# Turning q and k by squares on VectorE instead of whole on TensorE, from the ninth attention block on

## The chip, the cores and the metric

The kernel runs on one core of a Trainium2 chip. The metric is the device time of one launch in microseconds. The median of three runs before the change is 1019.25 us (1018.29 to 1020.09). A profile of one execution is read beside it; in it, all times count from the start of that execution's span.

## What is computed

Four batches of eight heads, 576 positions and 64 features per head go through window attention, and its output, 2304 tokens of 512 features, through two gated MLPs one after the other.

```python
scores = scale * np.matmul(q, k.transpose(0, 1, 3, 2))
mask = (rel >= 0) & (rel < 64)            # rel = query position - key position
attn = softmax(np.where(mask, scores, -1e9))
x = attn @ v                              # then (B, H, S, D) -> (B*S, H*D)
x = (silu(x @ w_gate) * (x @ w_val)) @ w_out
out = (sigmoid(x @ w2_gate) * (x @ w2_val)) @ w2_out
```

Everything is held to float32. The weights are 512 x 1536 and 1536 x 512 and arrive as float64 words, which the kernel rounds on the chip.

## The kernel before

The tokens are cut into 18 attention blocks of 128 tokens, numbered from 0, and into five tiles of 4, 3, 4, 4 and 3 blocks (`BLOCKS`). A tile of four blocks gives products of 512 columns, a tile of three blocks 384. The first MLP goes over the five tiles in turn, then the second MLP does. Each pass over a tile has twelve feature chunks, and each chunk three **slots**: the gate product (`g`, L402), the value product (`v`, L402) and the output product of the chunk before (`a`, L414). A product is twelve matmuls, since both operands are split into a high and a low float32r part. There are 36 slots to a tile, 360 in all.

The order around the products is written out by hand: three tables, `before`, `during` and `after`, hold for every slot what is issued ahead of its product, behind it and at its end. The instructions of each engine then run in that order, and each waits only for its operands and buffers. The attention of the first tile's blocks is done ahead of all products (`START`). The attention of every later block is spread over the slots of the tile before it by `plan_attention(i, base, ...)`; `base` is a gate slot, and the blocks of a tile are 9 or 12 slots apart. For one block it plans:

- slot `base - 2`: `load_qk`, the block's q and k, 128 tokens by 8 heads by 64 features each, from main memory into one buffer each (pool `nat`);
- `base + 1`, `base + 5`: v of the block, and a second tile `v0` that `pair_v` puts together by two copies within on-chip memory, from the v tiles of this block and the one before;
- ahead of the value product of slot `base + 1`: `transpose_in` for q and for k. Each is four TensorE transposes of 128 x 128 against an identity matrix (L183), into a PSUM bank. `evacuate` copies them out on ScalarE into `qt` (L192) and `kt` (L198); `kt` has 64 keys more, copied from the block before (L198);
- ahead of slot `base + 2`: the scores, 32 small matmuls (L217) that read `qt` and `kt`; then mask, exponentials and normalization, the transposes of the probabilities (L275), the product with v (L291) in slot `base + 9` or `base + 10`, and its split into the next tile's input (`x_hi` on ScalarE L301, `x_lo` on VectorE L304).

`qt` and `v0` share one buffer: `v0` of a block waits for its scores, and `qt` of the next block for this block's product with v. Weights come as 512 KB pieces (`raw`, L332) into four buffers; ScalarE (L350, L353) and VectorE (L361 to L364) round them. All of the first MLP's are rounded during the first tile's slots, slots 0 to 35, those of the second during tiles 2 and 3. Nearly all transfers are issued by SyncE's queue (SP), in order.

Of the kernel before, what the change touches and what calls it, by code (L numbers as in the profile page):

```python
# [8 lines left out]
FP32 = mybir.dt.float32  # L9
# [9 lines left out]
# A float64's upper word, read as a float32, for the magnitudes 2**-127 and about 2**128.  # L19
# [3 lines left out]
# What comes before the products, in order. Loads: q, k, v and the block, r and the last of the  # L23
# weight chunks whose words are wanted by then, h for the q and k of the next tile's first block.
# [3 lines left out]
# Steps: two letters, then the block (attention) or the chunk (c., weights).  # L28
# [11 lines left out]
def attention_moe_moe(  # L40
# [32 lines left out]
    ORDER2 = [t for t in range(NTL) if t != last] + [last]  # L73
    TILES = []
# [38 lines left out]
    def load_tokens(src, nm, t0, pool):  # L113
        pool, tag = pool or (nat_p, nm)
        t = pool.tile([128, H, D], FP32, tag=tag, name=nm)
        for off, n, b, s in runs(t0, 128):
            nc.sync.dma_start(
                out=t[off:off + n], in_=src[b, :, s:s + n, :].rearrange("h p d -> p h d")
            )
        return t  # L120

    def load_qk(i, pool=None):
        nat[i, "q"] = load_tokens(q, "q", 128 * i, pool)
        nat[i, "k"] = load_tokens(k, "k", 128 * i, pool)
# [4 lines left out]
    def pair_v(i, pool=None):  # L129
        """The keys of the block's first half, then those of the half block before them."""  # L130
        pool, tag = pool or (qt_p, "qt")
        q_eng = nc.scalar if early[0] else nc.sync
        t = pool.tile([128, H, D], FP32, tag=tag, name="v0")
        q_eng.dma_start(out=t[0:W], in_=nat[i, "v1"][0:W])
        if i:
            q_eng.dma_start(out=t[W:], in_=nat[i - 1, "v1"][W:])
        else:
            nc.gpsimd.memset(t[W:], 0.0)
        nat[i, "v0"] = t
# [4 lines left out]
    def make_masks():  # L144
        for nm, firsts in (("n", ()), ("a", (0,)), ("b", (1,))):
            m = const.tile([128, 2 * W], FP32, name=f"mask_{nm}")
            nc.vector.memset(m, 0.0)
            for half in range(2):
                mh = m[half * W:(half + 1) * W]
                own, before = (slice(0, W), slice(W, 2 * W))[::1 - 2 * half]  # L150
# [37 lines left out]
    def evacuate(i, nm):  # L188
# [4 lines left out]
        else:  # L193
# [5 lines left out]
            if i == 0:  # L199
                nc.gpsimd.memset(t[:, :, 128:], 0.0)  # L200
            else:
                copy(t[:, :, 128:], st[i - 1, "kt"][:, :, W:128])
            copy(t[:, :, 0:128], ps)
        st[i, nm + "t"] = t

    def scores(i, picks=(None, None), pars=(0, 1)):
        """A quarter of the array per product, four different ones in a row."""
# [3 lines left out]
        thirds = kt.rearrange("p a (g w) -> p a g w", w=W)  # L211
        for hp in range(HP):
            for par, half in ((0, 0), (0, 1), (1, 0), (1, 1)):
                if par not in pars:
# [5 lines left out]
                    rhs=kt[r, hp, 0:2 * W] if half else thirds[r, hp, 0:3:2, :],  # L220
# [63 lines left out]
    def pv(i, pick=None):  # L284
        ps = bank(pick)
        pt = [st.pop((i, "pt", par)) for par in range(2)]
        vv = [nat.pop((i, "v0")), nat[i, "v1"]]
# [29 lines left out]
    def rows(key):  # L317
        """The part of a weight that one tile holds, its features on the partitions."""
# [21 lines left out]
    # A float64 is rounded to a float32 as the sum of two words. One is the upper word without  # L340
# [121 lines left out]
    def plan_attention(i, base, t, col):  # L462
# [250 lines left out]
```

## Time and profile before

| | before |
|---|---|
| median of three runs | 1019.25 us |
| the profiled execution's span | 1017.5 us |
| TensorE busy in the span | 992.6 us, 98% |
| VectorE, ScalarE busy | 501.9 us, 509.1 us |
| mean granted TensorE clock | 0.984 |
| packets moved by DMA | 115285, 106.21 MB |

The span is the time from the first to the last instruction of one execution. The timed runs include what lies around it, and the median stands 1.75 us above the span. Busy shares are means over stages that differ: in the first 155 us the weights are rounded beside the first tile, and the last half of the run is products alone.

### The profile page before, as it was taken

To read this page: it belongs to the slowest core of one execution; us is meant where nothing else is said; L and a number is where in the kernel's file an instruction comes from. 1 tells how busy PE (TensorE), PEld (TensorE's weight loads), DVE (VectorE), ACT (ScalarE), POOL (GpSimd) and SP (SyncE) were. 2 spreads that over 40 slices of the span, in tenths; PEclk is the share of its full clock that TensorE was granted. 3 is DMA by queue.
4 is the path that set the end of the run, shared out by engine and by line. 5 is a ranking of instruction groups with operands and counts; after the bars stand their busy time and mean duration, and the time that the engine had idled before them with its cause. 6 is when DMAs were issued, how large, how long until landed. Compare 5 with 4: busy or idle time off the path is not lost.

```text
span 1017.5 us, 14797 instructions
## 1 busy us (share of the span) xinstructions
PE 992.6 (98%) x5701; PEld 855.2 (84%) x5701; DVE 501.9 (49%) x1161; ACT 509.1 (50%) x1011; POOL 4.1 (0%) x20
## 2 busy tenths in 40 slices
PE   8799998999999999999999999999999999999998
PEld 6677777999878888888999888899988888888997
DVE  6899994444466766666555422233322222222322
ACT  6899994665676777657444322222222222222222
POOL 1000000000000000000000000000000000000000
PEclk7799999999999999999999999999999999999999
DMA  9647664622176665564555310020020002000100
GB/s 227 183 156 210 196 196 134 177 74 73 44 226 197 177 197 190 185 206 145 189 153 157 135 41 1 1 83 1 1 73 1 0 1 73 1 1 1 42 1 32
DMA packets 115285, 106.21 MB, mean 104 GB/s; under 512 B 61008, under 2 KB 87632, under 8 KB 115216
## 3 DMA queue, kind: packets, MB, share of 16 engines
q1 hardware_dynamic: 114656, 104.36, 34.5%
q10 hardware_dynamic: 560, 0.92, 0.4%
q8 instruction: 45, 0.74, 0.3%
q14 instruction: 24, 0.20, 0.1%
HBM read 78.64 MB, written 22.02 MB: 99 GB/s over the span
## 4 chain that ended last, share of the span: by engine, by line
PE 83%; ACT 10%; DVE 4%; issue 2%; DMA 0%; ACTq 0%; SPq 0%; DVEq 0%
PE a L414 26%; PE g L402 26%; PE v L402 25%; ACT raw L350 3%; ACT z L252 2%; PE att L291 1%; PE att L183 1%; PE att L217 1%; ACT t L353 1%; PE att L275 1%; DVE raw L361 1%; DVE t L363 1%; ACT wv L384 1%; ACT L252 1%; ACT wg L384 0%
## 5 line engine op out<-in xcount | busy, mean ns | idle before, releaser
L402 PE MATMUL g<-x,wg 128*128 128x512 f32 (+1 forms) x1440 | 319.6, 371 | 1.3 <-ACT x L301 1.3
L402 PE MATMUL v<-x,wv 128*128 128x512 f32 (+1 forms) x1440 | 318.4, 369 | 0.0
L402 PEld LDWEIGHTS g<-x,wg 128*128 128x128 f32 x1440 | 264.7, 189 | 38.6 <-ACT x L301 1.4
L402 PEld LDWEIGHTS v<-x,wv 128*128 128x128 f32 x1440 | 260.6, 188 | 32.6
L666 DVE TENSOR_TENSOR s<-s,v 128x512 f32<-128x512 f32 (+1 forms) x120 | 76.0, 633 | 339.7 <-PE v L402 323.5
L657 ACT ACTIVATE s<-g 128x512 f32<-128x512 f32 (+1 forms) x120 | 66.6, 555 | 303.7 <-PE g L402 303.4
L414 PE MATMUL a<-h,wo 128*128 128x512 f32 (+1 forms) x720 | 164.9, 377 | 6.4 <-DVE h L582 6.4
L414 PE MATMUL a<-wo,h 128*128 128x512 f32 x648 | 157.5, 391 | 0.0
L668 ACT ACTIVATE h<-s 128x512 fp32r<-128x512 f32 (+1 forms) x120 | 70.6, 588 | 167.6 <-DVE s L666 167.6
L414 PEld LDWEIGHTS a<-h,wo 128*128 128x128 f32 x720 | 131.1, 190 | 26.7 <-DVE h L582 7.7
L414 PEld LDWEIGHTS a<-wo,h 128*128 128x128 f32 x648 | 121.3, 188 | 24.1
L350 ACT ACTIVATE raw<-raw 128x512 uint16<-128x512 uint32 x72 | 97.9, 1360 | 0.0
L582 DVE TENSOR_TENSOR h<-s,h 128x512 fp32r<-128x512 f32 (+1 forms) x120 | 76.2, 635 | 3.2
L361 DVE TENSOR_SCALAR raw<-raw 128x512 uint16<-128x512 uint16 x72 | 54.2, 752 | 17.4 <-ACT raw L350 17.3
L252 ACT ACTIVATE z<-z,nm 128x128 f32<-128x128 f32 x144 | 55.8, 390 | 2.9 <-DVE nm L236 2.7
L100 DVE TENSOR_TENSOR x<-rx,x 128x512 fp32r<-128x512 f32 (+1 forms) x20 | 12.8, 639 | 84.6 <-ACT x L99 84.6
L364 DVE CUSTOM_DVE_ANT_0 t<-raw,t 128x1024 uint16<-128x1024 uint16 x72 | 49.9, 693 | 2.5
L353 ACT ACTIVATE t<-raw 128x512 f32<-128x512 f32 x72 | 51.1, 710 | 0.0
L388 DVE TENSOR_TENSOR wo<-stay,wo 128x512 fp32r<-128x512 f32 x60 | 41.1, 685 | 0.0
L384 ACT ACTIVATE wo<-stay 128x512 fp32r<-128x512 f32 x60 | 37.4, 623 | 0.0
L388 DVE TENSOR_TENSOR wo<-tw,wo 128x512 fp32r<-128x512 f32 x48 | 33.0, 687 | 5.7 <-ACT wo L384 5.7
L362 DVE TENSOR_SCALAR t<-t 128x512 f32<-128x512 f32 x72 | 33.5, 465 | 0.0
(82 smaller groups left out, 588.9 us busy)
## 6 DMA issues: line engine op xcount, KB each, us to landing
raw<-in_moe_w_gate_dram SPq DMA_DIRECT2D x24, 512.0 KB, 4.2
raw<-in_moe_w_val_dram SPq DMA_DIRECT2D x24, 512.0 KB, 4.0
raw<-in_moe_w_out_dram SPq DMA_DIRECT2D x24, 512.0 KB, 3.7
tw<-k0o SPq DMA_DIRECT2D x48, 256.0 KB, 4.4
out_dram<-o SPq DMA_DIRECT2D x18, 256.0 KB, 2.3
k<-in_k_dram SPq DMA_DIRECT2D x16, 256.0 KB, 5.1
q<-in_q_dram SPq DMA_DIRECT2D x16, 256.0 KB, 4.7
v<-in_v_dram SPq DMA_DIRECT2D x16, 256.0 KB, 5.1
```

The costliest lines, as they stand in the source:

```text
L252: nc.scalar.activation(out=z[:, hp, :], in_=z[:, hp, :], func=ACTF.Exp, scale=-1.0, bias=nm[:, hp:hp + 1], accum_out=su[:, hp:hp + 1],)
L350: nc.scalar.activation(out=first, in_=lower.bitcast(UINT32), func=ACTF.Copy, scale=2.0 ** -29)
L353: nc.scalar.activation(out=t.bitcast(FP32), in_=upper.bitcast(FP32), func=ACTF.Abs)
L361: nc.vector.tensor_scalar(second, fourth, 0x8000, 0x4000, ALU.bitwise_and, ALU.bitwise_or)
L364: nc.vector.tensor_tensor(out=t, in0=t, in1=lower, op=ALU.add)
L388: nc.vector.tensor_tensor(out=w[:, 1], in0=mids.pop(key), in1=w[:, 0].bitcast(FP32), op=ALU.subtract)
L402: nc.tensor.matmul(out=ps[:, 0:n], lhsT=w[:, a, c, :], rhs=xt[:, b, c, 0:n], start=(j == 0), stop=(j == len(mm) - 1),)
L414: nc.tensor.matmul(out=acc[e][:, 0:n] if m == 0 else acc[e], lhsT=w[:, a, cols] if m == 0 else h[:, a, cols], rhs=h[:, b, 0:n] if m == 0 e ...
L582: nc.vector.tensor_tensor(out=h[:, 1, 0:n], in0=s, in1=h[:, 0, 0:n].bitcast(FP32), op=ALU.subtract)
L657: nc.scalar.activation(out=s, in_=gps[:, 0:n], func=(ACTF.Silu, ACTF.Sigmoid)[m])
L666: nc.vector.tensor_tensor(out=s, in0=s, in1=vps[:, 0:n], op=ALU.mult)
L668: nc.scalar.activation(out=h[:, 0, 0:n], in_=s, func=ACTF.Copy)
```

## The change

Blocks 0 to 7 keep their TensorE transposes. For blocks 8 to 17 (`TURN` is 8), the tokens that they need are first copied within main memory: `to_squares` copies q and k in pieces of 32 features of one token into two arrays, `squares`, in which the 32 x 32 squares of the transposed layout stand where the whole transposed matrix would have them, each square still unturned. There are 96 such transfers: 32 of 32 x 6 pieces (batch 1, from its position 384 on), in slots 12 to 27; 32 of 32 x 18 pieces (batch 2) in slots 24 to 39; 32 of 32 x 18 (batch 3) in slots 46 to 61. A piece is 32 float32 values, 128 bytes. All are issued by SP, ahead of what else its slot issues.

The block's `load_qk` then reads q as 128 partitions by four runs of 512 bytes and k, with the 64 keys before the block, as four runs of 768 bytes. In slot `base + 1`, `turn` makes `qt` and `kt` by one VectorE transpose each, 128 x 512 and 128 x 768, which turns every 32 x 32 square in its place. The transposes on TensorE and the three copies out of PSUM on ScalarE fall away for these blocks.

Besides, for all blocks, `load_before` loads `v0` from main memory (128 tokens by 8 heads by 64 features) in place of the two on-chip copies, the older keys now come first in `kt`, and so in the masks and in `v0`.

```diff
+    TURN = BLOCKS[0] + BLOCKS[1] + 1
...
+    squares = {nm: dram.tile([128, HP, NT // 32, 32], FP32, name=f"{nm}s") for nm in "qk"}
+
+    def to_squares(nm, b, s, hp, par):
+        src = {"q": q, "k": k}[nm][b, 2 * hp + par, s:S]
+        for a in range(2):
+            r0 = 64 * par + 32 * a
+            nc.sync.dma_start(
+                out=squares[nm][r0:r0 + 32, hp, (b * S + s) // 32:(b + 1) * S // 32, :],
+                in_=src[:, 32 * a:32 * a + 32].rearrange("(t r) d -> r t d", r=32),
+            )
+
     def load_qk(i, pool=None):
...
+        for nm, n in (("q", 4), ("k", 6)):
+            t = nat_p.tile([128, HP, n, 32], FP32, tag=nm, name=nm)
+            nc.sync.dma_start(out=t, in_=squares[nm][:, :, 4 * i + 4 - n:4 * i + 4, :])
+            nat[i, nm] = t
...
-        t = pool.tile([128, H, D], FP32, tag=tag, name="v0")
-        q_eng.dma_start(out=t[0:W], in_=nat[i, "v1"][0:W])
         if i:
-            q_eng.dma_start(out=t[W:], in_=nat[i - 1, "v1"][W:])
+            nat[i, "v0"] = load_tokens(v, "v0", 128 * i - W, pool, 0, eng)
...
+    def turn(i, nm):
+        src = nat.pop((i, nm)).rearrange("p a t c -> p a (t c)")
+        if nm == "q":
+            t = qt_p.tile([128, HP, 128], FP32, tag="qt", name="qt")
+        else:
+            t = kt_p.tile([128, HP, W + 128], FP32, tag="kt", name="kt")
+        nc.vector.transpose(t, src)
+        st[i, nm + "t"] = t
...
         for nm in "qk":
-            at(before, base + 1, transpose_in, i, nm)
-            at(before, base + 1, evacuate, i, nm)
+            if i < TURN:
+                at(before, base + 1, transpose_in, i, nm)
+                at(before, base + 1, evacuate, i, nm)
+            else:
+                at(before, base + 1, turn, i, nm)
...
+    for b in range(B):
+        s = max(0, 128 * TURN - W - b * S)
+        if s >= S:
+            continue
+        parts = [(nm, b, s, hp, par) for hp in range(HP) for par in range(2) for nm in "kq"]
+        first = {1: 12, 2: 24, 3: 46}[b]
+        for j, part in enumerate(parts):
+            at(during, first + j, to_squares, *part)
```

Three places show how the instructions move. On TensorE, around slot 43, in which block 8 is turned, the order before is (`att` is a PSUM bank, `ident` the identity matrix):

```order
L402 MATMUL g<-x,wg 128x384 x12
L183 MATMUL att<-ident,q 128x128 x4
L183 MATMUL att<-ident,k 128x128 x4
L402 MATMUL v<-x,wv 128x384 x12
L217 MATMUL att<-kt,qt 64x128 x16
```

and in the changed kernel (L429 is the products' line there, L441 the output product's, L244 the scores'):

```order
L429 MATMUL g<-x,wg 128x384 x12
L429 MATMUL v<-x,wv 128x384 x12
L244 MATMUL att<-kt,qt 64x128 x16
L441 MATMUL a_2123<-h,wo 128x384 x3
L441 MATMUL a_2124<-h,wo 128x384 x3
```

The two rows of transposes are gone, there and in nine later blocks, and the value product follows the gate product at once.

On VectorE, in slot 79, in which block 12 is turned, the order before is (L364 is the last step of a weight's rounding, L582 the low half of the hidden values, L304 `x_lo`, L666 the gate times the value product, L361 the next weight's rounding):

```order
L364 ISA t<-raw,t 128x1024
L582 TENSOR_TENSOR h<-s,h 128x512
L304 TENSOR_TENSOR x<-att,x 128x4x128
L666 TENSOR_TENSOR s<-s,v 128x512
L361 TENSOR_SCALAR raw<-raw 128x512
```

and in the changed kernel (the same steps are L621, L331 and L705 there):

```order
L621 TENSOR_TENSOR h<-s,h 128x512
L331 TENSOR_TENSOR x<-att,x 128x4x128
L231 STREAM_TRANSPOSE qt<-q 128x512
L231 STREAM_TRANSPOSE kt<-k 128x768
L705 TENSOR_TENSOR s<-s,v 128x512
```

The two transposes have come in between `x_lo` of block 11 and the instruction that waits for the value product.

On SP, in slots 24 and 25, where transfers of two batches are issued in the same slots, the order before is (`k0o` is a rounded weight on its way to main memory):

```order
L332 DMA raw<-in_moe_w_out_dram 128x1024
L370 DMA k0o_1517<-t 128x512
L332 DMA raw<-in_moe_w_gate_dram 128x4x256
L117 DMA v<-in_v_dram 128x8x64
L332 DMA raw<-in_moe_w_val_dram 128x4x256
```

and in the changed kernel (`ks` and `qs` are the arrays of squares):

```order
L359 DMA raw<-in_moe_w_out_dram 128x1024
L133 DMA ks<-in_k_dram 32x6x32 x2
L133 DMA ks<-in_k_dram 32x18x32 x2
L397 DMA k0o_1542<-t 128x512
L359 DMA raw<-in_moe_w_gate_dram 128x4x256
L133 DMA qs<-in_q_dram 32x6x32 x2
L133 DMA qs<-in_q_dram 32x18x32 x2
L118 DMA v<-in_v_dram 128x8x64
L359 DMA raw<-in_moe_w_val_dram 128x4x256
```

Four transfers of squares now stand ahead of the other transfers in each of these slots.

## Rows read from the trace of the kernel before

**Rows 1.** The page: engines' busy time and share; DMA busy tenths in 40 slices.

```profile
PE 992.6 (98%) x5701; PEld 855.2 (84%) x5701; DVE 501.9 (49%) x1161; ACT 509.1 (50%) x1011; POOL 4.1 (0%) x20
...
DMA  9647664622176665564555310020020002000100
```

**Rows 2.** The page: the chain that ended last, shares of the span by engine.

```profile
PE 83%; ACT 10%; DVE 4%; issue 2%; DMA 0%; ACTq 0%; SPq 0%; DVEq 0%
```

**Rows 3.** Stretches 186 to 264 and 264 to 455: engines' busy us, clock, DMA share, GB/s.

```profile
186.00:264.00 78.00, 78.00 (x664) 74.97 (x659) 32.09 (x114) 42.74 (x106) 0.00 (x0) 1.00 0.34 89
264.00:455.00 191.00, 189.39 (x1197) 154.26 (x1196) 124.87 (x313) 137.74 (x268) 0.00 (x0) 1.00 0.63 188
```

**Rows 4.** Waits of TensorE from 175 to 470 us: us in total, times, longest.

```profile
PE att L183 <- ACT qt L192: 0.7, 1, 0.7
```

**Rows 5.** Timeline of TensorE in slot 118: start us, us.

```profile
411.27 0.60 PE L183 MATMUL att<-ident,q 128*128 128x128 f32 x4
411.70 0.60 PE L183 MATMUL att<-ident,k 128*128 128x128 f32 x4
412.06 2.98 PE L402 MATMUL v<-x,wv 128*128 128x512 f32 x12
```

**Rows 6.** Timeline around slot 79, block 12.

```profile
285.54 0.66 PE L183 MATMUL att<-ident,q 128*128 128x128 f32 x4
...
286.71 0.69 DVE L304 TENSOR_TENSOR x<-att,x 128x512 fp32r<-128x512 f32 x1
...
287.29 3.00 PE L402 MATMUL v<-x,wv 128*128 128x512 f32 x12
...
290.22 1.10 PE L217 MATMUL att<-kt,qt 64*64 64x128 f32 x32
```

**Rows 7.** Lines of VectorE, shapes apart: busy us, mean ns.

```profile
L582 DVE TENSOR_TENSOR h<-s,h 128x512 fp32r<-128x512 f32 x72 | 49.6, 689 | 3.2
...
L582 DVE TENSOR_TENSOR h<-s,h 128x384 fp32r<-128x384 f32 x48 | 26.6, 554 | 0.0
```

**Rows 8.** Timeline, slots 43 and 97: VectorE's last work ahead, and the scores.

```profile
187.94 0.55 DVE L582 TENSOR_TENSOR h<-s,h 128x384 fp32r<-128x384 f32 x1
...
191.83 1.10 PE L217 MATMUL att<-kt,qt 64*64 64x128 f32 x32
...
345.65 0.69 DVE L582 TENSOR_TENSOR h<-s,h 128x512 fp32r<-128x512 f32 x1
...
348.45 1.10 PE L217 MATMUL att<-kt,qt 64*64 64x128 f32 x32
```

**Rows 9.** DMA from 3 to 6.5 us, q and k alone in 256-byte pieces.

```profile
DMA packets 3256, 0.82 MB, mean 234 GB/s; under 512 B 3256, under 2 KB 3256, under 8 KB 3256
```

**Rows 10.** Three stretches of slots 24 to 28, 29 to 35 and 46 to 61.

```profile
124.00:142.00 18.00, 15.83 (x101) 12.57 (x100) 17.59 (x41) 15.88 (x25) 0.00 (x0) 1.00 0.78 220
142.00:171.00 29.00, 26.01 (x167) 20.34 (x166) 21.13 (x60) 18.92 (x40) 0.00 (x0) 0.94 0.62 182
198.00:239.00 41.00, 41.00 (x349) 39.33 (x348) 16.30 (x47) 25.48 (x65) 0.00 (x0) 1.00 0.29 76
```

**Rows 11.** A weight piece: its issue, its first use, and landing times of such pieces.

```profile
132.24 0.38 SPq L332 DMA_DIRECT2D raw<-in_moe_w_gate_dram  x1
...
139.00 1.38 ACT L350 ACTIVATE raw<-raw 128x512 uint16<-128x512 uint32 x1
...
DMA to landing us min/median/max: 3.3/3.7/4.7
```

**Rows 12.** k of block 10: its issue on SP, and its transposes on TensorE.

```profile
217.87 0.70 SPq L117 DMA_DIRECT2D k<-in_k_dram  x1
...
235.25 0.60 PE L183 MATMUL att<-ident,k 128*128 128x128 f32 x4
```

**Rows 13.** The page, DMA issues: count, KB each, median us to landing.

```profile
v<-in_v_dram SPq DMA_DIRECT2D x16, 256.0 KB, 5.1
v<-v SPq DMA_DIRECT2D x28, 128.0 KB, 3.9
```

More of the change, by code (lines that the diff above doesn't have):

```diff
@@ L111, in attention_moe_moe, with load_tokens @@
     nat = {}
-    def load_tokens(src, nm, t0, pool):
+    def load_tokens(src, nm, t0, pool, at=0, eng=nc.sync):
         pool, tag = pool or (nat_p, nm)
         t = pool.tile([128, H, D], FP32, tag=tag, name=nm)
-        for off, n, b, s in runs(t0, 128):
-            nc.sync.dma_start(
-                out=t[off:off + n], in_=src[b, :, s:s + n, :].rearrange("h p d -> p h d")
-            )
-        return t
-    def load_qk(i, pool=None):
-        nat[i, "q"] = load_tokens(q, "q", 128 * i, pool)
-        nat[i, "k"] = load_tokens(k, "k", 128 * i, pool)
+        for off, n, b, s in runs(t0, 128 - at):
+            eng.dma_start(
+                out=t[at + off:at + off + n], in_=src[b, :, s:s + n, :].rearrange("h p d -> p h d")
+            )
+        return t
@@ new lines, in attention_moe_moe @@
+    squares = {nm: dram.tile([128, HP, NT // 32, 32], FP32, name=f"{nm}s") for nm in "qk"}
[7 more added lines that the diff above has]
+            )
+    def load_qk(i, pool=None):
+        if i < TURN:
+            nat[i, "q"] = load_tokens(q, "q", 128 * i, pool)
+            nat[i, "k"] = load_tokens(k, "k", 128 * i, pool)
+            return
+        for nm, n in (("q", 4), ("k", 6)):
+            t = nat_p.tile([128, HP, n, 32], FP32, tag=nm, name=nm)
+            nc.sync.dma_start(out=t, in_=squares[nm][:, :, 4 * i + 4 - n:4 * i + 4, :])
+            nat[i, nm] = t
@@ L137, in pair_v @@
         else:
-            nc.gpsimd.memset(t[W:], 0.0)
-        nat[i, "v0"] = t
+            nat[i, "v0"] = load_tokens(v, "v0", 0, pool, W, eng)
+            nc.gpsimd.memset(nat[i, "v0"][0:W], 0.0)
     ident = const.tile([128, 128], FP32, name="ident")
@@ L149, in make_masks @@
                 mh = m[half * W:(half + 1) * W]
-                own, before = (slice(0, W), slice(W, 2 * W))[::1 - 2 * half]
+                before, own = slice(0, W), slice(W, 2 * W)
                 nc.gpsimd.affine_select(
@@ L199, in evacuate @@
             if i == 0:
-                nc.gpsimd.memset(t[:, :, 128:], 0.0)
+                nc.gpsimd.memset(t[:, :, 0:W], 0.0)
             else:
-                copy(t[:, :, 128:], st[i - 1, "kt"][:, :, W:128])
-            copy(t[:, :, 0:128], ps)
+                copy(t[:, :, 0:W], st[i - 1, "kt"][:, :, 128:])
+            copy(t[:, :, W:], ps)
+        st[i, nm + "t"] = t
[6 more added lines that the diff above has]
+        nc.vector.transpose(t, src)
         st[i, nm + "t"] = t
@@ L210, in scores @@
         qt, kt = st[i, "qt"], st[i, "kt"]
-        thirds = kt.rearrange("p a (g w) -> p a g w", w=W)
         for hp in range(HP):
@@ L219, in scores @@
                     lhsT=qt[r, hp, half * W:(half + 1) * W],
-                    rhs=kt[r, hp, 0:2 * W] if half else thirds[r, hp, 0:3:2, :],
+                    rhs=kt[r, hp, half * W:(half + 2) * W],
                     start=True,
@@ L466, in plan_attention @@
         at(during, base + 1, load_v, i)
-        at(during, base + 5, pair_v, i)
+        at(during, base + 5, load_before, i)
         for nm in "qk":
-            at(before, base + 1, transpose_in, i, nm)
-            at(before, base + 1, evacuate, i, nm)
+            if i < TURN:
+                at(before, base + 1, transpose_in, i, nm)
+                at(before, base + 1, evacuate, i, nm)
+            else:
+                at(before, base + 1, turn, i, nm)
         at(before, base + 2, scores, i)
```

9 lines of the change are left out of this document (4 added, 5 removed).

## The prediction

> **What bounds the kernel now.** I read the page first. TensorE is busy for 992.6 of 1017.5 us [rows 1], and the chain of work that ended last runs on it for 83% of the span [rows 2]. Then I asked for the stretch in which the blocks to be changed are turned, 186 to 455 us. [...] VectorE is busy there for 32.09 of 78 and 124.87 of 191 us, ScalarE for more [rows 3]. Of TensorE's few waits there, one is due to the part that is removed: 0.7 us, once, for `qt` [rows 4].
>
> The first tile, up to about 171 us, is another matter. From 124 to 142 us VectorE is busy for 17.59 of 18.00 us and the DMA engines for 0.78 [rows 10]: rounding the weights and loading them leave little room, and the new transfers of batches 1 and 2 begin in just this stage.
>
> **What is removed.** Ten blocks lose eight TensorE transposes each. What they cost is not their busy time, since matmuls overlap, but the distance from the start of the first to the start of the product behind: 412.06 - 411.27 = 0.79 us [rows 5]. Ten times that is 7.9 us. In block 12's slot the same distance is 287.29 - 285.54 = 1.75 us [rows 6], because the second four waited for ScalarE's copy; so another 0.96 us. In sum 8.9 us. The three ScalarE copies per block go too. I cost that at nothing: they lay beside products, and TensorE waited for them only in the place just counted. If ScalarE had been the bound there, this would be a gain that I leave out.
>
> **What is added on VectorE.** Two transposes per block, over 512 and 768 elements per partition. The trace has no such instruction. The nearest rows are float32 instructions with one result per element and lane: 689 ns for 512 elements and 554 for 384 [rows 7], so 1.05 ns per element and, for 768, 0.69 + 256 x 0.00105 = 0.96 us. Back to back such instructions start some 0.08 us before the one ahead ends; I take 0.61 + 0.96 = 1.57 us for the pair. As bounds I take half of that, 0.8 us, if two elements pass at a time, and twice, 3.1 us, if a 4-byte element needs two passes. I take the middle value because the data is of the same width and length as in the rows.
>
> Who waits? The transposes stand in VectorE's order behind the low half of the hidden values (or `x_lo`), and the scores need both. In slot 43 VectorE is done at 188.49, and the scores would start at 191.83 - 0.79 = 191.04: 2.55 us of room [rows 8]. In slot 97 it is done at 346.34 and the scores would start at 347.66: 1.32 us, a wait of 0.25 [rows 8]. In slot 79, `x_lo` ends at 287.40 and the scores would start at 290.22 - 1.75 = 288.47: 1.07 us, a wait of 0.5 [rows 6]. The other seven have between 1.5 and 2.6 us of room, as I read them. Behind the transposes on VectorE queues the product of gate and value (L666 before), which waits for TensorE's value product anyway and so is not late. I count 0.75 us of new waits.
>
> [...]
>
> **What is added on the DMA engines.** The squares are 32 x 192 + 64 x 576 = 43008 pieces of 128 bytes, each read from main memory and written to it. No row shows such a copy. The nearest is a stretch with 256-byte pieces alone: 3256 in 3.5 us over 16 engines, 17.2 ns each per engine [rows 9]. If bytes decided, a piece would take 8.6 ns; if read and write were both a piece's full price, 34.4. [...] Over the run that is 43008 x 17.2 / 16 = 46 us of all engines (23 to 92). The ten q and k loads come in longer runs than before, and `v0` in 256-byte pieces from main memory in place of on-chip copies; a load of that kind lands after 5.1 us and the copy after 3.9 [rows 13], four slots before use, so I cost that at nothing. Should the cover fail, it costs the late landing, about a microsecond per block.
>
> Where does it bind? In slots 24 to 28 there are 10 x 576 + 8 x 192 = 7296 pieces, 7.8 us of engine time, and 0.22 x 18 = 4.0 us free [rows 10]: the queue runs 3.9 us late by 142 us. A weight piece there is issued at 132.24, lands after 3.7 and is used at 139.00 [rows 11]: 3.1 us of room, when by its landing at 136 two thirds of the lateness, 2.6 us, have built up. Behind 142 us, 8064 pieces take 8.7 of 0.38 x 29 = 11.0 us free [rows 10], and no piece of the first tile's weights is urgent any more. I count 0.5 us lost in the first tile. In slots 46 to 61, 18432 pieces take 19.8 us of 0.71 x 41 = 29.1 free [rows 10]. What could be late there are loads of q and k, but SP issues them far ahead: 217.87 for a use at 235.25, 12 us of room beyond a landing of 5.1, which a load of that size takes [rows 12, 13]. On SP each transfer costs about 0.4 us to issue, between the 0.38 of a weight piece [rows 11] and the 0.70 of k [rows 12], four to a slot of 18 / 5 = 3.6 us at most; SP waits for VectorE in that stage, so this lies under its wait.
>
> **The sum.** 7.9 + 0.96 - 0.75 - 0.5 = 7.6 us off the profiled execution, 1017.5 to 1009.9. The median of the runs stands 1.75 us above that span, and I carry this over: 1011.6 us.
>
> **The rivals.** *The copies choke the DMA engines (the other side).* At 34.4 ns a piece, slots 24 to 28 ask for 15.7 us where 4.0 are free, and weight pieces arrive 11.7 - 3.1 = 8.6 us too late for a ScalarE and a VectorE that have no slack there; slots 46 to 61 ask for 39.6 where 29.1 are free, and with 12 us of room they pay about a microsecond. The sum is 8.9 - 0.75 - 9.6 = 1.5 us slower: 1021. It decides from about 31 ns a piece; at 50 it would be near 1040. For it speaks the full DMA row in the first tile, against it that 256-byte pieces cost only 17.2. Chance 0.16.
>
> [...] The trace shows 256-byte pieces at 234 GB/s [rows 9] and no copy in smaller ones.
>
> *The transposes take twice as long.* At 3.1 us the ten blocks' scores wait 0.6 us four times and between 1.1 and 2.1 us six times, 11.7 us in all, which is 1022.6. For it: nothing in the trace; against it: all float32 rows of that length stand between 0.4 and 0.7 us. Chance 0.06.
>
> *Part of the gain is eaten.* The copies cost about 25 ns a piece, or the SP queue blocks while the engines are full, and the first tile loses 3 to 5 us: 1014 to 1017. Chance 0.13.
>
> *The work removed was not on the path.* Then the time stays at 1019. The row of TensorE, full to 189.39 of 191.00 us, speaks against it. Chance 0.05.
>
> **How the numbers follow.** My forecast, 1009 to 1014 for its own bounds (no DMA loss and no score waits at the one end, 3 us of DMA loss at the other), has 0.60. The range of 1008 to 1022 takes in the eaten gain, the unchanged time, the slower transposes in part and the milder half of the choked copies. About 0.2% (2 us) is what a measurement of this kernel can tell from no change. Faster by more: 0.60 + 0.13 = 0.73, less 0.01 for an eaten gain at its end: 0.72. Within it: the unchanged 0.05, that 0.01, and 0.05 from the mildest parts of the two slower rivals: 0.11. Slower, the rest of those two: 0.17.
>
> **What would show it.** Right: L183 rows only for blocks 0 to 7; in tiles 1 to 3 the value product of slot `base + 1` starts 2.1 or 2.7 us after the gate product; waits of TensorE's scores for `kt` under 0.6 us each; transposes at about 0.69 and 0.96 us; packets of 128 bytes at about 17 ns with the DMA row at 9 from 124 to 145 us; first-tile slots ending no more than a microsecond later than before. Wrong: ScalarE's rounding (L350 before) waiting for its `raw` transfer; SP issue times over a microsecond in slots 24 to 40; scores waiting over a microsecond in many blocks.

## The result and the profile after

The changed kernel runs in 1010.43 us, the median of four runs (1009.91 to 1010.98), against 1019.16 before; the ratio is 0.9915, with a 95% interval of 0.9904 to 0.9927. That is 8.7 us faster; forecast were 7.6. The profiled execution's span is 1009.2 us (1017.5 before), at a mean granted clock of 0.983.

The page of the changed kernel: engines' busy time, the DMA engines' busy tenths in 40 slices, packets, and the chain that ended last ([rows 1, 2] are the same lines of before).

```profile
PE 984.6 (98%) x5621; PEld 847.7 (84%) x5621; DVE 516.4 (51%) x1181; ACT 496.7 (49%) x981; POOL 4.1 (0%) x20
...
DMA  9647798773176666573644400020020002000100
...
DMA packets 164982, 113.03 MB, mean 112 GB/s; under 512 B 102704, under 2 KB 139568, under 8 KB 164912
...
PE 80%; DVE 7%; ACT 7%; issue 3%; SPq 2%; DMA 1%; DVEq 0%; ACTq 0%
```

TensorE has 80 instructions and 8.0 us of busy time less, VectorE 20 instructions and 14.5 us more, ScalarE 30 instructions and 12.4 us less. The chain has SPq on it now, the issuing of transfers by SP, with 2%; 18.3 us of it lie before 20 us, ahead of the first copy, so it is no sign of the copies.

The new VectorE instructions, with the shortest, the median and the longest in ns:

```profile
L231 DVE STREAM_TRANSPOSE qt<-q x10: 701/705/712, 188.8 to 439.9; 128x512 f32<-128x512 f32 x10
L231 DVE STREAM_TRANSPOSE kt<-k x10: 933/936/979, 190.3 to 440.7; 128x768 f32<-128x768 f32 x10
```

Where the gain lies can be read from the timeline, by the time from the start of one slot's product to the start of the next. The two kernels' slots agree to 0.06 us, but for a few in the first tile and these, in us:

| block | gate slot, before and after | value slot, before and after | gain |
|---|---|---|---|
| 8 | 2.98, 2.19 | 3.30, 3.22 | 0.87 |
| 9, 10, 11, each | 2.98, 2.19 | 3.30, 3.21 | 0.88 |
| 12 (slots 78, 79) | 5.65, 3.89 | 3.96, 4.53 | 1.19 |
| 13, 15, each | 3.65, 2.85 | 3.94, 3.85 | 0.89 |
| 14 (slots 96, 97) | 3.67, 2.86 | 3.94, 4.26 | 0.49 |
| 16, 17, each | 3.52, 2.72 | 3.94, 3.85 | 0.89 |

That is 8.75 us. From the start of slot 36 to that of slot 132 it is 285.02 us before and 276.21 after, 8.81; from there to the last product 553.09 in both. From the first product to slot 36 it is 128.15 and 128.20: the first tile loses 0.05. The first product itself starts at 43.52 in place of 43.15; more on that below.

The wait that the transposes bring stands in two of the ten value slots. The waits of TensorE from 175 to 470 us in the changed kernel (total, times, longest; [rows 4] for before):

```profile
PE att L302 <- DVE z L294: 0.9, 2, 0.6
PE att L244 <- DVE kt L231: 0.8, 2, 0.5
```

and the timeline of slot 79 (start, duration; [rows 6] for before):

```profile
282.44 0.69 DVE L391 CUSTOM_DVE_ANT_0 t<-raw,t 128x1024 uint16<-128x1024 uint16 x1
282.47 3.02 PE L429 MATMUL v<-x,wv 128*128 128x512 f32 x12
...
283.06 0.69 DVE L621 TENSOR_TENSOR h<-s,h 128x512 fp32r<-128x512 f32 x1
...
283.66 0.68 DVE L331 TENSOR_TENSOR x<-att,x 128x512 fp32r<-128x512 f32 x1
...
284.26 0.70 DVE L231 STREAM_TRANSPOSE qt<-q 128x512 f32<-128x512 f32 x1
284.88 0.94 DVE L231 STREAM_TRANSPOSE kt<-k 128x768 f32<-128x768 f32 x1
...
285.96 1.10 PE L244 MATMUL att<-kt,qt 64*64 64x128 f32 x32 [0.48 <-DVE kt L231]
```

VectorE works from 282.44 to 285.82 without a gap; the value product is through at about 285.5, and the scores start 0.48 us later, when `kt` is there.

In slot 43, block 8's, TensorE does not wait, but only just. VectorE is ready for k 0.72 us before it has landed (in brackets: idle time and what ended it), and the scores start 0.14 us after `kt` is done:

```profile
190.26 0.98 DVE L231 STREAM_TRANSPOSE kt<-k 128x768 f32<-128x768 f32 x1 [0.72 <-DMA k<-ks]
...
191.38 1.10 PE L244 MATMUL att<-kt,qt 64*64 64x128 f32 x32
```

The stretches of slots 24 to 28 and 29 to 35 (columns as in [rows 10], which has 0.78 and 0.62 as the DMA engines' share):

```profile
124.00:142.00 18.00, 15.94 (x100) 12.56 (x99) 17.59 (x40) 15.94 (x25) 0.00 (x0) 1.00 0.90 231
142.00:171.00 29.00, 25.92 (x166) 20.28 (x165) 20.93 (x58) 19.18 (x40) 0.00 (x0) 0.94 0.95 231
```

The DMA engines' share is up to 0.90 and 0.95, and yet TensorE, VectorE and ScalarE have done the same work there as before, to 0.3 us. The share adds up the times of the packets, and it has no ceiling at 1: in the stretch of [rows 9] it is 1.31. So 0.95 does not say that nothing more would fit.

### The profile page after: what moved, and what is told of

Read it like the earlier page. It is cut to its first block, busy times and chain, and to the rows that moved or that the text cites. A ratio compares the mean times of both kernels' runs of the same rounds, so it can differ in the third digit from the quotient of the medians.

```text
span 1009.2 us, 14684 instructions
## 1 busy us (share of the span) xinstructions
PE 984.6 (98%) x5621; PEld 847.7 (84%) x5621; DVE 516.4 (51%) x1181; ACT 496.7 (49%) x981; POOL 4.1 (0%) x20
## 4 chain that ended last, share of the span: by engine, by line
PE 80%; DVE 7%; ACT 7%; issue 3%; SPq 2%; DMA 1%; DVEq 0%; ACTq 0%
PE a L441 26%; PE g L429 26%; PE v L429 24%; ACT raw L377 2%; SPq L118 2%; ACT z L279 1%; DVE raw L388 1%; PE att L244 1%; PE att L318 1%; DVE t L390 1%; PE att L302 1%; DMA ks<-in_k_dram 1%; ACT L279 1%; DVE t L389 1%; DVE s L705 1%
## 5 line engine op out<-in xcount | busy, mean ns | idle before, releaser
L429 PE MATMUL g<-x,wg 128*128 128x512 f32 (+1 forms) x1440 | 319.5, 370 | 0.7 <-ACT x L328 0.7
L429 PE MATMUL v<-x,wv 128*128 128x512 f32 (+1 forms) x1440 | 317.6, 369 | 0.0
L429 PEld LDWEIGHTS g<-x,wg 128*128 128x128 f32 x1440 | 264.6, 189 | 38.0 <-ACT x L328 0.9
L429 PEld LDWEIGHTS v<-x,wv 128*128 128x128 f32 x1440 | 261.2, 188 | 33.0
L705 DVE TENSOR_TENSOR s<-s,v 128x512 f32<-128x512 f32 (+1 forms) x120 | 75.9, 632 | 314.7 <-PE v L429 303.6
L441 PE MATMUL a<-h,wo 128*128 128x512 f32 (+1 forms) x720 | 164.8, 377 | 6.3 <-DVE h L621 6.3
L441 PE MATMUL a<-wo,h 128*128 128x512 f32 x648 | 157.4, 390 | 0.0
L441 PEld LDWEIGHTS a<-h,wo 128*128 128x128 f32 x720 | 131.2, 190 | 26.5 <-DVE h L621 7.6
L441 PEld LDWEIGHTS a<-wo,h 128*128 128x128 f32 x648 | 121.3, 188 | 24.2
L621 DVE TENSOR_TENSOR h<-s,h 128x512 fp32r<-128x512 f32 (+1 forms) x120 | 76.2, 635 | 3.2
L388 DVE TENSOR_SCALAR raw<-raw 128x512 uint16<-128x512 uint16 x72 | 53.9, 748 | 17.4 <-ACT raw L377 17.3
```

What stands on the lines that cost most here:

```text
L388: nc.vector.tensor_scalar(second, fourth, 0x8000, 0x4000, ALU.bitwise_and, ALU.bitwise_or)
L429: nc.tensor.matmul(out=ps[:, 0:n], lhsT=w[:, a, c, :], rhs=xt[:, b, c, 0:n], start=(j == 0), stop=(j == len(mm) - 1),)
L441: nc.tensor.matmul(out=acc[e][:, 0:n] if m == 0 else acc[e], lhsT=w[:, a, cols] if m == 0 else h[:, a, cols], rhs=h[:, b, 0:n] if m == 0 e ...
L621: nc.vector.tensor_tensor(out=h[:, 1, 0:n], in0=s, in1=h[:, 0, 0:n].bitcast(FP32), op=ALU.subtract)
L705: nc.vector.tensor_tensor(out=s, in0=s, in1=vps[:, 0:n], op=ALU.mult)
```

## The experiments

The theory: each block gives back TensorE's time for eight transposes; the copies and VectorE's transposes just fit beside the products. The rivals: the copies choke the DMA engines and hide part of the gain; the VectorE transposes are free or costly; the gain comes from ScalarE or from `v0`. Each median stands beside runs of the kernel before on the same chip, whose medians are 1019.29 to 1019.37. "Slots" are starts of products read from the timeline of each profiled execution.

| kernel | median us | ratio to before, interval |
|---|---|---|
| v0 alone | 1019.94 | 1.0008 (0.9999 to 1.0017) |
| copies alone | 1020.60 | 1.0013 (1.0004 to 1.0022) |
| turned from block 12 | 1014.36 | 0.9952 (0.9940 to 0.9965) |
| v0 on the chip | 1010.01 | 0.9918 (0.9906 to 0.9931) |
| turned twice | 1020.18 | 1.0007 (0.9997 to 1.0016) |
| copied twice | 1039.91 | 1.0209 (1.0195 to 1.0223) |
| small twins | 1030.82 | 1.0107 (1.0091 to 1.0122) |
| direct loads | 1063.86 | 1.0445 (1.0427 to 1.0463) |
| ScalarE's copies kept | 1011.13 | 0.9919 (0.9905 to 0.9932) |
| k early | 1012.74 | 0.9936 (0.9923 to 0.9949) |
| k and its load early | 1009.47 | 0.9904 (0.9891 to 0.9918) |
| the same, from block 7 | 1007.75 | 0.9894 (0.9879 to 0.9909) |

**v0 and the keys' order alone; the copies alone.**

```diff
-    TURN = BLOCKS[0] + BLOCKS[1] + 1
+    TURN = sum(BLOCKS)
```

> The changed kernel without squares: every block is turned on TensorE, nothing is copied in main memory; what stays is v0 from main memory and the older keys first in kt. Theory (these cost 0.5 us ahead of the first product, where the changed kernel's first product stood 0.55 us later than before, and nothing later): 1019.2 + 0.5 = 1019.7 us, first product at 43.7. Rival (the 0.55 us come from the squares or are chance): 1019.2, first product at 43.15. Second rival (v0 from main memory frees something in every block, so part of the 8.7 us comes from it): below 1018.

One thing is not as expected there: some copies are left. With `TURN` at 18 the loop still copies the last 64 positions of batch 3, since 128 x 18 - 64 - 3 x 576 = 512 is below 576: 32 transfers of 64 pieces, in slots 46 to 61 (count, KB each, median us to landing):

```profile
ks<-in_k_dram SPq DMA_DIRECT2D x16, 8.0 KB, 2.2
```

The kernel with copies alone has the same line and, so that they are still issued:

```diff
-        s = max(0, 128 * TURN - W - b * S)
+        s = max(0, 128 * (BLOCKS[0] + BLOCKS[1] + 1) - W - b * S)
```

> As the kernel with v0 alone, but the 96 copies into squares are issued in their slots and nothing reads them. The difference to that kernel is the price of the copies by themselves. Theory (they fill the DMA engines from 124 to 171 us, but no weight piece comes late enough): 0 to 0.5 us more, 1019.7 to 1020.2. Rival (copies choke the DMA engines, and the gain on TensorE hides part of it in the changed kernel): 2 us or more, 1022 and above.

v0 alone is 0.6 us above before with an interval that reaches to no change; from the first product to the last its slots take 966.20 us, before 966.26. So from the first product on neither v0 from main memory nor the 32 small copies cost anything. The first product starts at 43.65 us, as the theory has it; whether v0 is the reason is tested below. The copies alone, with 64 transfers and 40960 pieces more, are 0.66 us above by the medians, 0.58 by the slots: 0.16 up to slot 36 and 0.33 in slot 42, the rest spread. The DMA engines are not choked.

What a piece costs is read from the same two kernels, in the stretch from 190 to 250 us, in which batch 3 is copied by 32 transfers in both, of 64 and of 576 pieces: first v0 alone, then copies alone (columns as in [rows 3]), and the packets of the stretch in the same order.

```profile
190.00:250.00 60.00, 60.00 (x484) 57.88 (x483) 24.07 (x88) 34.48 (x92) 0.00 (x0) 1.00 0.42 103
```

```profile
190.00:250.00 60.00, 59.87 (x483) 57.78 (x483) 23.61 (x88) 34.29 (x92) 0.00 (x0) 1.00 0.66 143
```

```profile
DMA packets 16528, 6.17 MB, mean 103 GB/s; under 512 B 15219, under 2 KB 15219, under 8 KB 16521
```

```profile
DMA packets 33594, 8.61 MB, mean 143 GB/s; under 512 B 32181, under 2 KB 32181, under 8 KB 33589
```

33594 - 16528 = 17066 packets more take (0.66 - 0.42) x 60 x 16 = 230 us of one engine more: 13.5 ns each. A copied piece shows as one packet of 128 bytes (the changed kernel's profile has 43008 of that size, the one before none); 16384 of the packets are pieces, the others belong to transfers that moved into the stretch, so this is an estimate.

**Turned from block 12 on.**

```diff
-    TURN = BLOCKS[0] + BLOCKS[1] + 1
+    TURN = 12
```

> Only blocks 12 to 17 are turned on VectorE, blocks 8 to 11 on TensorE as before; the copies start at the 64 keys ahead of block 12, so batch 1 is not copied at all. Theory (each block gives back 0.79 us of TensorE): 4 x 0.79 = 3.2 us more than the changed kernel, less 0.3 for the copies that fall away: 1013.3. Rival (most of the gain comes from ScalarE being freed, or from the one wait in slot 79, not from TensorE's time per block): within 1 us of the changed kernel, 1010.4 to 1011.4.

The time is 3.9 us above the changed kernel; from slot 36 to slot 132 the slots take 279.70 in place of 276.21, 3.49 us for four blocks or 0.87 each. The rival is out: the gain goes with the number of blocks. It also shows why a block is worth 0.88 and not 0.79. In the kernel with v0 alone, slot 118, with the transposes:

```profile
411.74 0.60 PE L202 MATMUL att<-ident,q 128*128 128x128 f32 x4
412.18 0.60 PE L202 MATMUL att<-ident,k 128*128 128x128 f32 x4
412.53 2.98 PE L429 MATMUL v<-x,wv 128*128 128x512 f32 x12
415.44 1.10 PE L244 MATMUL att<-kt,qt 64*64 64x128 f32 x32
```

and in the changed kernel the same slot:

```profile
404.68 2.88 PE L429 MATMUL v<-x,wv 128*128 128x512 f32 x12
407.49 1.10 PE L244 MATMUL att<-kt,qt 64*64 64x128 f32 x32
```

Start to start the product takes 2.91 us behind transposes and 2.81 behind a product: it starts while the transposes still run, and seems to pay the 0.1 us inside itself; that the overlap is the reason is a reading of these rows, which no run tests by itself. The older keys' place is not the cause, since v0 alone has it too.

**v0 on the chip.**

```diff
...
+        eng.dma_start(out=t[W:], in_=nat[i, "v1"][0:W])
         if i:
-            nat[i, "v0"] = load_tokens(v, "v0", 128 * i - W, pool, 0, eng)
+            eng.dma_start(out=t[0:W], in_=nat[i - 1, "v1"][W:])
...
```

> The changed kernel with v0 put together by two copies within on-chip memory, as before; all else as changed. Theory (v0 from main memory costs 0.5 us ahead of the first product): 1010.4 - 0.5 = 1009.9, first product at 43.15. Rival (the 0.55 us come from elsewhere): 1010.4, first product at 43.7.

1010.01, 0.4 us below the changed kernel with intervals that overlap widely. But the first product starts at 43.74 us, not at 43.15: my reason for the 0.5 us is wrong. By its slots the kernel is 0.7 us slower from the first product on, 0.50 of it in slot 43, where the scores wait for `kt` because block 8's k lands late.

**Each VectorE transpose twice.**

```diff
         nc.vector.transpose(t, src)
+        nc.vector.transpose(t, src)
```

> The changed kernel with each VectorE transpose issued twice, one behind the other, into the same tile: 3.3 us of VectorE per block in place of 1.65. In the changed kernel the second transpose ends 0.0 to 2.3 us ahead of the time at which TensorE comes to the scores; by these distances, block by block (1.65 + 3 x 0.8 + 1.65 + 0 + 1.65 + 0 + 0.15 + 0), theory (only the distance to the scores counts) expects 7.5 us of new waits: 1018, with waits of TensorE for kt in seven blocks and none in blocks 13, 15 and 17. Rival (VectorE transposes cost little even when doubled, since VectorE is idle half of the time): under 2 us, below 1012.5.

Waits of TensorE from 175 to 470 us:

```profile
PE att L245 <- DVE kt L232: 7.8, 6, 2.2
```

7.8 us in six blocks. 0.8 of them were there before, so 7.0 us are new, against 7.5 expected in seven blocks. The largest difference is in slot 43, with a wait of 0.86 where 1.65 was expected; otherwise the distances to the scores were read rightly to about 0.15 us, and VectorE's half-empty time does not help. The median rose by 9.75 us; in the profiled execution slots 36 to 131 take 8.99 more. Of what the new waits don't account for there, 1.45 us stand in slot 80, behind the longest of them. The output product there waits for nothing, but it runs at a lower clock (columns as in [rows 3]; the wait of 2.24 us ends at 289.83):

```profile
291.00:295.40 4.40, 4.40 (x16) 3.52 (x14) 4.33 (x22) 1.62 (x2) 0.00 (x0) 0.65 0.45 139
295.40:300.00 4.60, 4.60 (x22) 3.80 (x21) 1.89 (x4) 1.70 (x2) 0.00 (x0) 1.00 0.44 133
```

0.65 is a mean: the clock records of the executions before and after the change hold two levels alone, 0.50 and 1.00 of full speed (in the changed kernel 0.50 from 28 to 33 us, 1.00 from 35 to 40). From 295.4 us on it is 1.00 again. In the changed kernel, whose wait there is 0.48 us, the same product takes 3.01 us. But a wait of this size is not enough by itself: in slot 97 of the same execution TensorE waits 2.11 us, and the output product behind takes no longer than usual, at a granted clock of 1.00.

```profile
350.02 1.10 PE L245 MATMUL att<-kt,qt 64*64 64x128 f32 x32 [2.11 <-DVE kt L232]
351.05 3.02 PE L442 MATMUL a<-h,wo 128*128 128x512 f32 x12
```

**Every copy twice; small twins.**

```diff
+    spare = {nm: dram.tile([128, HP, NT // 32, 32], FP32, name=f"{nm}s2") for nm in "qk"}
...
-            nc.sync.dma_start(
+            for to in (squares, spare):
+                nc.sync.dma_start(
...
```

> The changed kernel with every copy into squares issued twice, the second into arrays that nothing reads: 192 transfers and 86016 pieces in the same slots. Theory (the changed kernel's copies just fit: DMA engines 0.90 and 0.95 busy from 124 to 171 us, SP 0.6 us per transfer): twice as many don't fit, the loads of q and k for block 8 and the weight pieces from slot 24 on come late, 3 to 8 us more, 1013.5 to 1018.5, with SP or the DMA engines named in the waits before slot 43. Rival (a piece costs 13 ns and the copies have room to spare): under 1 us more, below 1011.5.

It costs 29.5 us, far more than I expected, 17.3 of them between the first product and slot 36. The DMA engines are not the main cause: in the stretch from 124 to 171 us their share is 0.93 in the changed kernel, and *less*, 0.82, with twice the copies. Here is the changed kernel, then the one with doubled copies:

```profile
124.00:171.00 47.00, 41.86 (x265) 32.84 (x264) 38.52 (x97) 35.12 (x64) 0.00 (x0) 0.96 0.93 231
```

```profile
124.00:171.00 47.00, 36.49 (x199) 28.45 (x198) 34.23 (x79) 31.88 (x57) 0.00 (x0) 0.89 0.82 192
```

What is full is SP: of these 47 us it waits for 36.1 in the kernel before, for 7.6 in the changed kernel, and for 3.0 with doubled copies. Its rows in the changed kernel, two transfers of 192 pieces and then two of 576:

```profile
90.68 1.22 SPq L133 DMA_DIRECT2D qs<-in_q_dram  x2
...
152.06 1.23 SPq L133 DMA_DIRECT2D ks<-in_k_dram  x2
```

and with doubled copies, eight in a slot:

```profile
131.83 5.17 SPq L135 DMA_DIRECT2D ks<-in_k_dram  x8
137.10 0.57 SPq L399 DMA_DIRECT2D k0o<-t  x1
137.76 0.39 SPq L361 DMA_DIRECT2D raw<-in_moe_w_gate_dram  x1
138.21 5.85 SPq L135 DMA_DIRECT2D qs<-in_q_dram  x8
144.10 0.62 SPq L118 DMA_DIRECT2D v<-in_v_dram  x1
```

In the changed kernel a copy takes 0.61 us to issue, of 192 pieces as of 576; here eight take more than a slot of 3.6 us, and weights, q, k and v queue behind. To tell this from the pieces I gave each copy a twin of 32 pieces:

```diff
...
+            nc.sync.dma_start(
+                out=spare[nm][r0:r0 + 32, hp, (b * S + s) // 32:(b * S + s) // 32 + 1, :],
+                in_=src[0:32, 32 * a:32 * a + 32].rearrange("(t r) d -> r t d", r=32),
+            )
```

> The changed kernel with a second transfer behind every copy, but one of 32 pieces only, into arrays that nothing reads: 192 transfers as in the kernel with doubled copies, and 43008 + 3072 pieces in place of 86016. It tells apart why doubled copies cost 29.5 us. Theory (SP is the limit: a transfer takes it 0.6 us to issue whether it has 192 or 576 pieces, and eight take 5 us of a slot of 3.6): most of the loss comes back, 1025 to 1040. Rival (the DMA engines are the limit, by pieces): 1010.4 to 1012.

With 7% more pieces and twice the transfers it loses 20.4 us, of which 14.0 before slot 36, with the DMA engines' share at 0.71 and SP's waits down to 2.2 us in the same stretch. A twin's row in it:

```profile
132.02 0.59 SPq L134 DMA_DIRECT2D ks<-in_k_dram  x1
132.66 0.60 SPq L138 DMA_DIRECT2D ks<-in_k_dram  x1
```

The second, with 32 pieces, costs SP as much as the first with 192 or 576. So 20.4 of the 29.5 us are the number of transfers; the other 9.1 go with the 39936 pieces that the doubled copies have above the twins.

**Direct loads, without copies.**

```diff
-            nc.sync.dma_start(out=t, in_=squares[nm][:, :, 4 * i + 4 - n:4 * i + 4, :])
+            for off, m, b, s in runs(128 * i + 128 - 32 * n, 32 * n):
+                for par in range(2):
+                    for a in range(2):
+                        r0 = 64 * par + 32 * a
+                        for hp in range(HP):
+                            src = {"q": q, "k": k}[nm][b, 2 * hp + par, s:s + m, 32 * a:32 * a + 32]
+                            nc.sync.dma_start(
+                                out=t[r0:r0 + 32, hp, off // 32:(off + m) // 32, :],
+                                in_=src.rearrange("(t r) d -> r t d", r=32),
+                            )
...
-            at(during, base - 2, load_qk, i)
+            at(during, base - (7 if i >= TURN else 2), load_qk, i)
...
```

The loop that issues the copies falls away.

> The changed kernel without copies in main memory: the ten blocks' q and k are loaded from the inputs into the squares' places at once, in pieces of 128 bytes, by 16 transfers for q and 16 or 32 for k, issued from slot base - 7 on in place of base - 2. The first tile is free of copies. Theory (the copies cost the changed kernel at most 0.5 us, and SP issues 32 transfers in 20 us, in time for base + 1): 1010.0 to 1010.5. Rival (SP's queue is blocked for 20 us in every block, and weight pieces or v behind it come late in the second and third tile): 2 us or more, above 1012.5.

The rival, and by far more than it said: 53 us above the changed kernel. SP's rows from 301 us on, and what TensorE waited for from 175 to 470 us:

```profile
301.18 17.02 SPq L151 DMA_DIRECT2D q<-in_q_dram  x32
318.30 15.00 SPq L151 DMA_DIRECT2D k<-in_k_dram  x32
```

```profile
PE att L327 <- DMA v<-in_v_dram: 38.7, 5, 19.4
```

These are the loads of block 13, which lies in two batches and so needs 32 transfers each for q and k; they hold SP for 32 us. In all it is 368 transfers, and v, which comes behind them, is up to 19.4 us late. The copies in main memory spare this: 96 transfers, and 20 to read the squares back.

**ScalarE's copies kept.**

```diff
         nc.vector.transpose(t, src)
         st[i, nm + "t"] = t
+        for part in ((src,) if nm == "q" else (src[:, :, 0:W], src[:, :, W:])):
+            nc.scalar.activation(out=part, in_=part, func=ACTF.Copy)
```

> The changed kernel with ScalarE's three copies per block put back (128x512 and 128x64x4 and 128x512, in place on the q and k tiles behind their transposes; the results are as before). Theory (the copies that fell away were worth nothing): 1010.4, within 0.5. Rival (ScalarE's freed 1.8 us per block carry part of the gain): 2 us or more, 1012.5 and above.

ScalarE's busy time is back, 510.4 us against 509.1 before, but not its old place: the copies stand behind the transposes, and the scores do not need them. 1011.13, 0.7 above the changed kernel with overlapping intervals; by the slots 0.44, of which 0.34 in slot 43, where block 8's k has no time to spare. In the other nine blocks they cost nothing. So ScalarE's time is worth nothing there; what its place between transposes and scores was worth is seen in block 12 alone, whose gate slot gains 0.97 us more than the others (5.65 to 3.89).

**k a slot earlier; with its load earlier; from block 7 on.**

```diff
-                at(before, base + 1, turn, i, nm)
+                at(before, base + (nm == "q" or i == TURN), turn, i, nm)
```

> The changed kernel with k turned one slot earlier, in slot base in place of base + 1, for blocks 9 to 17; q stays, since its tile is shared with v0. Theory (slots 79 and 97 lose 0.56 and 0.32 us because both transposes stand between x_lo or the low half and the scores): those waits fall away, 0.9 us less, 1009.5. Rival (the scores wait there for something else, as x_lo or a PSUM bank, that stands ahead of the transposes anyway): 1010.4, waits as before.

1012.74: 2.3 us above the changed kernel by the medians, 3.38 from slot 36 to slot 132. In slot 78 VectorE now stands before a k that has not landed, and all that follows it on VectorE is late; behind the wait of 2.17 us the output product again runs at a lower clock, 0.67, and slot 80 takes 4.17 us in place of 2.85. The numbers in brackets are idle time and what ended it:

```profile
281.02 0.98 DVE L231 STREAM_TRANSPOSE kt<-k 128x768 f32<-128x768 f32 x1 [3.54 <-DMA k<-ks]
...
285.20 0.70 DVE L231 STREAM_TRANSPOSE qt<-q 128x512 f32<-128x512 f32 x1
...
286.05 1.36 PE L244 MATMUL att<-kt,qt 64*64 64x128 f32 x32 [2.17 <-DVE qt L231]
```

So the next one also loads earlier:

```diff
-            at(during, base - 2, load_qk, i)
+            at(during, base - (2 if i <= TURN else 5), load_qk, i)
```

> The kernel with k turned a slot earlier, whose VectorE waited 3.54 us for k's landing in slot 78, with the loads of q and k of blocks 9 to 17 issued in slot base - 5 in place of base - 2. Theory (that kernel failed by the landing of k alone): k's transpose falls into VectorE's idle time, the scores' waits in slots 79, 80 and 97 fall away, 0.9 us less than the changed kernel: 1009.5. Rival (VectorE has a backlog there by its own work, and a transpose put earlier only delays the rounding and what follows): 1010.4 or above, with waits for qt or kt of 0.3 us and more left in both slots.

1009.47. In slot 78 and 79 the theory holds: k is turned in VectorE's idle time, and the scores follow the product without a wait.

```profile
279.17 0.97 DVE L231 STREAM_TRANSPOSE kt<-k 128x768 f32<-128x768 f32 x1
...
284.40 0.70 DVE L231 STREAM_TRANSPOSE qt<-q 128x512 f32<-128x512 f32 x1
...
285.56 1.10 PE L244 MATMUL att<-kt,qt 64*64 64x128 f32 x32
```

In slot 97 the rival holds: the scores still wait 0.34 us, now for `qt`, behind VectorE's own rounding. From slot 36 to slot 132 it is 275.69 us, 0.52 less than the changed kernel; the timed 0.96 agrees with that within the intervals.

The last has `TURN = 7` besides:

> The same with block 7 turned on VectorE as well, whose slot lies at the end of the first tile, and batch 1 copied from its position 256 on (10 pieces in a row of a transfer in place of 6, as many transfers). Theory (a block gives back 0.88 us; 4096 pieces more cost nothing, since SP's issues stay as many): 0.9 us below the kernel with early loads, 1008.6. Rival (slots 24 to 35 wait for the DMA engines, VectorE and ScalarE and not for TensorE, so a block turned there gives nothing, and more pieces cost): same or up to 2 us slower.

The fastest median, 1007.75, 11.6 us below before; but its interval overlaps that of the one above, and its profile does not show the gain. In the profiled execution, the slowest of its runs (1011.28), block 7's `kt` waits for k, whose transfer took 6.4 us to land there, and the scores wait 2.74 us:

```profile
165.92 0.98 DVE L231 STREAM_TRANSPOSE kt<-k 128x768 f32<-128x768 f32 x1 [2.50 <-DMA k<-ks]
...
167.05 1.70 PE L244 MATMUL att<-kt,qt 64*64 64x128 f32 x32 [2.74 <-DVE kt L231]
```

Whether the other runs had k in time stays open.

## Why the prediction was right, point by point

- **What is removed.** Right in place, a little small in size. The 0.79 us ahead of the product were there in each of the ten blocks (0.79 to 0.81), and the 0.96 of block 12 too (5.65 to 3.89 is 1.76, 0.97 above its 0.79). What the term left out is the 0.08 to 0.10 us that the product behind paid for running into the transposes, 0.71 us in eight blocks. The distance was read from the first transpose to the product; read to the start of the scores, and set against a product that follows another product, it would have had this. Counting TensorE's time one for one as time off the end held: from 186 to 455 us TensorE was busy for 267.39 of 269 us at a granted clock of 1.00 [rows 3], and what the slots give back is the timed gain to 0.03 us (below).
- **ScalarE's copies at nothing.** Right: put back beside the products, they cost 0.4 us, nearly all in slot 43.
- **VectorE's transposes.** 0.70 and 0.94 us against 0.69 and 0.96: taking the row of a float32 instruction of that length was right. The pair takes 1.65 us. From 512 to 768 elements a transpose grows by 0.23 us, 0.9 ns per element, which leaves about 0.24 us fixed in each.
- **Who waits.** 0.5 us in slot 79 and 0.25 in slot 97 were forecast, 0.48 and 0.34 are there, and none in the other eight. Slot 43 is among those eight by luck: the forecast gave its transposes 2.55 us of room by VectorE's order alone, and took k's early landing from block 10. Block 8's k was issued at 182.54 before, 6.7 us ahead of its use, of which a landing takes 5.1; in the changed kernel SP comes to it at 184.61, it lands 0.72 us late for VectorE, and 0.14 us are left at the scores. The doubled transposes show how near the others stand: 1.65 us more per block brings 7.0 us of new waits.
- **The first tile, 0.5 us.** Too large: the copies alone cost 0.16 us up to slot 36, and in the changed kernel 0.05 is lost there. That the copies alone cost 0.58 in all is near the forecast by luck, since 0.33 of it stand in slot 42, in the second tile. The price per piece was too high: 13.5 ns and not 17.2, 36 us of all engines and not 46. That a copied piece of 128 bytes costs as much as a loaded one of 256 was my estimate; no run shows it, and the runs show 13.5 in its place. And the 4.0 us that were called free read the DMA engines' share as if it could not pass 1, which it does in [rows 9], at 1.31; how much room there was is not known from it. The rival with 34.4 ns was wrong by its price, which no row shows for copies in 128-byte pieces.
- **SP's queue.** This was the wrong step, though it did no harm: 0.4 us per transfer, hidden in SP's waits. It is 0.61, by the number of transfers more than of pieces, and SP's waits from 124 to 171 us shrink from 36.1 to 7.6 us; the copies still fit, with little to spare. SP is what would bind first. The choked rival had named the DMA engines, and only the eaten gain had SP's queue beside them, but twice the transfers fill SP, with a smaller share of the engines than before: 0.71 with the twins and 0.82 with doubled copies, against 0.93.
- **v0.** Nothing, as forecast. The later first product is not its doing: it starts at 43.52 us in the changed kernel, 43.74 with v0 put together on the chip, 42.38 in the kernel turned from block 12, which starts with the same instructions as the changed one.
- **The sum.** By the slots: 7.96 us for the transposes, 0.97 for the wait in block 12, 0.71 in the products behind, less 0.89 in slots 79 and 97 and 0.05 in the first tile, 8.70; the timed gain is 8.73. The forecast of 7.6 is short by the 0.71 and by most of the 0.5; the mechanism was right, and no large errors cancel in it.

## What to carry to other kernels

What an instruction on a full TensorE is worth is the change in the distance between two unaffected starts on either side of it (0.88 us a block here), not its own busy time (eight transposes of 0.27 us each) and not the distance to the next start alone (0.79 us). Work moved to a half-idle engine is free only where its place in that engine's order leaves time until its reader (VectorE's transposes brought waits of 0.48 and 0.34 us in two of ten blocks, and none in the others): read that distance block by block, and remember that a transpose put earlier needs its load earlier as well (without that VectorE stood 3.54 us before a k that had not landed). When many small transfers are added, count the transfers on the issuing queue (about 0.6 us of SP for each copy here) as well as the pieces on the DMA engines (13.5 ns each); a hand-made rearrangement in main memory pays when it turns many loads in small pieces into few, as here 368 into 96 copies and 20 loads, which are 53 us faster.

## What the runs showed of the hardware

- A copy within main memory in pieces of 128 bytes cost about 13.5 ns of one engine per piece, by packet time. The 256-byte pieces into on-chip memory of [rows 9] come to 22.5 ns by that measure (1.31 x 3.5 x 16 us over 3256), and to 17.2 ns by elapsed time, since packets of one engine overlap there.
- A wait of TensorE of some 2 us can cost more than itself: behind waits of 2.24 and 2.17 us in slot 79 the next output product, with all operands there, took 4.46 and 4.33 us in place of 3.01, at a mean clock of 0.65 and 0.67. Behind a wait of 2.11 us in slot 97 it took 3.02 us at 1.00, and behind the 0.48 us of the changed kernel 3.01. What decides between them stays open.
- Issuing a copy within main memory took SP about 0.6 us for 32, 192 or 576 pieces alike (medians 0.59 to 0.63); the direct loads into on-chip memory, of 64 to 192 such pieces, took 0.43 to 0.44. With doubled copies SP is nearly solid with issues from 124 to 171 us, waiting for 3.0 of 47 us, with the DMA engines' share at 0.82.
- Executions differ ahead of the first product, where these kernels have the same work: from 0 to 43 us the granted clock is 0.73 in the changed kernel and 0.90 in the one turned from block 12, and the first product starts at 43.52 and 42.38. The clock alone does not settle the start: with direct loads it is 0.76 and the start 42.40, before the change 0.76 and 43.15. In order, the changed kernel and the one turned from block 12:

```profile
0.00:43.00 43.00, 35.20 (x333) 28.23 (x333) 31.82 (x125) 33.31 (x96) 4.08 (x20) 0.73 0.90 205
```

```profile
0.00:43.00 43.00, 29.89 (x335) 23.84 (x336) 32.28 (x127) 34.33 (x98) 4.08 (x20) 0.90 0.89 207
```

So differences of about a microsecond between single executions were read slot by slot here, from the first product on. In the first tile even this is no sharper than some 0.5 us between executions that start so differently: up to slot 36 the kernel turned from block 12 takes 127.52 us and the one with k early 127.70, against 128.20.
